# A smaller mask product, separate keys for the first transfers, and a planner without its correction tables

## The chip, the cores and the metric

The kernel runs on one core of a Trainium2 chip. The metric is the device time of one execution in microseconds (us). Three executions of the kernel before took 328.57, 328.97 and 334.71 us, median 328.97. One more execution was taken with the hardware profiler; all rows below are from it.

## The reference

Two independent layers are computed and put side by side into an output of 2048 rows and 1280 columns, all in bf16.

```python
# A: 640 channels, 2048 steps
k_shift = sum(k_pad[:, t:t+S, :] * shift_k[:, ks-1-t] for t in range(4))
kv = k_shift * v
y = causal_long_convolution(kv, ssm_k)      # written with rfft/irfft of length 4096
a = q * (y + kv * ssm_D)
# B: 32 heads of 20, 4 segments of 512 steps
for s in range(4):
    p = softmax(qs @ ks.T * scale + causal_mask)
    a_dot = p @ vs
    a_mem = (phi(qs) @ M) / (phi(qs) @ z + 1e-6)      # phi(t) = t+1 if t>0 else exp(t)
    outs.append(g * a_mem + (1 - g) * a_dot)
    M, z = M + phi(ks).T @ vs, z + phi(ks).sum()
b = concat(outs) @ wo
return concat([a, b], axis=-1)
```

## The kernel before, in words

**Part A** runs over five blocks of 128 channels (`a_chunks(dp)`). For each block the filter `sk` and the keys are loaded, `sk` is turned by products with the identity (`turn`), the keys are shifted by products with `skd` (`kshift`), both are transformed by products with the table `Wf` (`fwd`, evicted by ScalarE into `F`), combined by VectorE (`bfly`, `pointwise`, `ybfly`: products and sums over tiles `Xh`, `Kh`, `S`), and transformed back by products with `Wi` (`inverse`), whose result VectorE multiplies by q into `outa` and GpSimd's queue writes out.

**Part B** runs over eight units: segment `s` = u // 2 and half of the heads u % 2. A unit's projection (`b_proj_chunks(u)`) multiplies `xT` (x transposed by a DMA) by `wqkv` for four tiles of 128 tokens, in the order K, Q, V. ScalarE casts K and Q into `KQ`; SyncE's queue (SP) transposes them by DMA into `KT` and `QT`, eight transposes per unit. `bound` then takes the largest absolute key on VectorE (`kam`), multiplies on TensorE, and writes a row `bT` into `QT` by a DMA. `mem` updates the state `Mbd`. A unit's attention (`b_attn_chunks(u)`) runs over four groups of four heads (`attn(g)`). For each group three score blocks are made one after the other in the one PSUM tile `st` (four banks, one per head); ScalarE takes the exponential of each into `ET`, of which there are three; VectorE multiplies the diagonal blocks of the first two by `cmask`; TensorE multiplies `ET` by `Va` into the one bank `o`; VectorE divides. When both halves of a segment are through, `o_s` is transposed by DMAs (`outt`) and multiplied by `wo` (`outproj`, evicted into `outb`).

The third score block holds key tile 3 in columns 0 to 127 and key tile 2 in columns 128 to 383. Before its score products, four products of the identity with `nmask` (two causal masks of -30000 and a block of zeros, 384 columns) put the mask into the four banks; the score products add to them. A score product works on 32 of TensorE's rows (`tile_position`), so that the four heads of a group run beside each other; I call these four a quartet.

**The order.** No call is issued as it is written. A recorder (`Proxy`, `Recorder.add`) collects the calls as operations, each with a key: `("A", block, stage)`, `("P", unit, stage)` for projections, `("T", unit, stage)` for attention and output, `("load", name)`, `("beta",)`, and `("const",)` for everything issued at set-up. Consecutive products into one bank are one operation. `Recorder.price` gives each an assumed duration. `plan` schedules them: it runs a list scheduler forward in time, then backward, up to seven forward runs, and keeps the shortest by its own durations. The first run's priorities are the length of the work behind an operation plus a correction per key from the table `BIAS`; in the later runs an eighth of that correction is kept. `HOLD` names, per key, a time before which a transfer isn't issued; in the later runs it moves the times that the planner derives for loads. `emit` then issues everything in the chosen order, so all instructions have the line of `emit` in the profile. Each engine, and each engine's DMA queue, works through its own instructions in that order. PSUM has one `st` of four banks, three banks `ab` and one bank `o`.

Of the kernel before, what the change touches and what calls it, by code (L numbers as in the profile page):

```python
# [12 lines left out]
bf16 = mybir.dt.bfloat16  # L13
# [80 lines left out]
class Recorder:  # L94
# [87 lines left out]
    def price(self, op, method, out, ins, kw):  # L182
        n = int(np.prod(list(out.shape)[1:]))
        two = lambda a: mybir.dt.size(a.dtype) == 2
        if method == "matmul":
            if "tile_position" in kw:
                op.dur += n / 2.4 * 0.33 + (200.0 if not op.dur else 0.0)
            else:
                op.dur += max(n / 2.4 + 2.5, 27.0)
# [15 lines left out]
        elif op.eng == "DVE":  # L205
            op.stall = 115 if method == "reciprocal" else 0
            fast = all(two(a) and a.space != bass.MemoryType.PSUM and int(a.ap[-1][0]) == 1 for a in [out] + ins)
            if method == "tensor_tensor":
                op.dur = n / (1.92 if fast else 0.96) + 60
            elif method == "tensor_reduce":  # L210
                op.dur = int(np.prod(list(ins[0].shape)[1:])) / 0.96 + 60
            elif method == "reciprocal":
                op.dur = 67 + 6.1 * n
            else:
                op.dur = n / (3.84 if fast else 1.9) + 60
            op.lat = 150.0
        else:
            op.dur, op.lat = 100 + n / 1.2, 200.0
# [231 lines left out]
class K3:  # L450
    def __init__(self, ctx, tc, A_q, A_k, A_v, A_shift_k, A_ssm_k, A_ssm_D, B_x, B_wq, B_wk, B_wv, B_wo, B_beta, out):
# [20 lines left out]
        def const(name, arr, dt, eng=nc.gpsimd):  # L472
            t = c.tile(list(arr.shape), dt, name=name)
# [8 lines left out]
        def wload(engs, half):  # L482
            def f():
                for i, (w, eng) in enumerate(zip((B_wk, B_wq, B_wv), engs)):
                    eng.dma_start(out=self.wqkv[:, :, half, i, :], in_=w.rearrange("(cc p) j -> p cc j", p=128)[:, :, 320 * half:320 * half + 320])
# [6 lines left out]
        }  # L492
        self.skc = c.tile([128, 5, 4], bf16, name="skc")
        nc.sync.dma_start(out=self.skc[:], in_=self.shift_k.rearrange("(c p) t -> p c t", p=128))
        self.ident = const("ident", np.eye(128).astype(BF16_NP), bf16, nc.sync)
        bt = self.bt = c.tile([128, H], bf16, name="bt")
# [4 lines left out]
        self.nmask = const("nmask", np.concatenate([(cmask_np.astype(np.float32) - 1) * 30000.0] * 2 + [np.zeros((128, 128), np.float32)], axis=1).astype(BF16_NP), bf16)  # L501
        self.epsrow = const("epsrow", eps_np, f32)

        self.KQ = c.tile([128, 2, 2, 16, 32], bf16, name="KQ")
        self.PK = c.tile([128, 4, 16, 32], bf16, name="PK")
# [45 lines left out]
    def a_chunks(self, dp):  # L551
# [22 lines left out]
        def load_kv():  # L574
            vt = st["vt"] = self.ring("vt", [128, 4, 4, 128])
            for b in range(4):
                nc.sync.dma_start(out=vt[:, b], in_=self.v[512 * b:512 * b + 512, dsl].rearrange("(p c) d -> p c d", c=4))
            kr = st["kr"] = self.ring("kr", [128, 4, KPAD + 512])
            nc.gpsimd.memset(kr[:, :, 0:KPAD], 0.0)
            for c in range(4):  # L580
                nc.sync.dma_start_transpose(out=kr[:, c, KPAD:KPAD + 512], in_=self.k[:, dsl].rearrange("(r c) d -> r c d", c=4)[:, c, :])
            skd = st["skd"] = self.ring("skd", [128, 4, 128])
# [191 lines left out]
    def b_attn_chunks(self, u):  # L774
# [6 lines left out]
        def attn(g):  # L781
            def f():
# [5 lines left out]
                for spec, e0, step in ((((0, 0),), 0, -1), (((1, 0),), 512, 1), (((3, 0), (2, 128)), 896, -1)):  # L788
                    st = self.bank("st")
                    masked = e0 == 896  # L790
                    if masked:
                        for hl in range(4):
                            nc.tensor.matmul(st[:, hl, 0:384], lhsT=self.ident[:], rhs=self.nmask[:], start=True, stop=False)
                    for (kc, c0) in spec:
                        for hl in range(4):
                            rows = slice(32 * hl, 32 * hl + 32)
                            nc.tensor.matmul(st[:, hl, c0:c0 + L - 128 * kc], lhsT=KT[rows, g, 128 * kc:128 * kc + 128], rhs=QT[rows, g, 128 * kc:L],
                                             start=not masked, stop=(not masked or kc == 2), tile_position=(32 * hl, 0))
# [82 lines left out]
    ('A', 0, 0): 157004, ('A', 0, 1): 10101, ('A', 0, 10): -7597, ('A', 0, 11): 3913, ('A', 0, 12): 33761, ('A', 0, 13): -3728, ('A', 0, 14): 5624,  # L881
    ('A', 0, 15): 88348, ('A', 0, 16): 230629, ('A', 0, 17): -8128, ('A', 0, 18): -5757, ('A', 0, 19): 10830, ('A', 0, 2): 8829, ('A', 0, 20): 4481,
    ('A', 0, 21): 1304, ('A', 0, 22): -3994, ('A', 0, 23): 145, ('A', 0, 24): -576, ('A', 0, 25): -2524, ('A', 0, 26): -1099, ('A', 0, 27): -2858,
    ('A', 0, 3): 16866, ('A', 0, 4): -698, ('A', 0, 5): -458, ('A', 0, 6): 389434, ('A', 0, 7): 607, ('A', 0, 8): 3517, ('A', 0, 9): -8145,
    ('A', 1, 0): -1731, ('A', 1, 1): 3601, ('A', 1, 10): -137531, ('A', 1, 11): -176854, ('A', 1, 12): -7874, ('A', 1, 13): -16279, ('A', 1, 14): 10588,
    ('A', 1, 15): 2905, ('A', 1, 16): -7, ('A', 1, 17): -2655, ('A', 1, 18): -2590, ('A', 1, 19): -1545, ('A', 1, 2): 1649, ('A', 1, 20): 40028,
    ('A', 1, 21): 1391, ('A', 1, 22): 3816, ('A', 1, 23): -2584, ('A', 1, 24): -7, ('A', 1, 25): -2923, ('A', 1, 26): 731, ('A', 1, 27): 396,
    ('A', 1, 3): 395, ('A', 1, 4): -322, ('A', 1, 5): 12977, ('A', 1, 6): 7861, ('A', 1, 7): -1057, ('A', 1, 8): -201, ('A', 1, 9): 261,
    ('A', 2, 0): -69696, ('A', 2, 1): -2356, ('A', 2, 10): -15708, ('A', 2, 11): 257, ('A', 2, 12): -55, ('A', 2, 13): 1762, ('A', 2, 14): 6674,
    ('A', 2, 15): 491, ('A', 2, 16): 243, ('A', 2, 17): -2104, ('A', 2, 18): 175, ('A', 2, 19): 3992, ('A', 2, 2): -3416, ('A', 2, 20): 250546,  # L890
    ('A', 2, 21): -2544, ('A', 2, 22): -615, ('A', 2, 23): -563, ('A', 2, 24): -3861, ('A', 2, 25): 952, ('A', 2, 26): 5253, ('A', 2, 27): -3491,
    ('A', 2, 3): -2503, ('A', 2, 4): -4457, ('A', 2, 5): 2480, ('A', 2, 6): 5034, ('A', 2, 7): -2075, ('A', 2, 8): 243, ('A', 2, 9): -346,
    ('A', 3, 0): -36045, ('A', 3, 1): 546, ('A', 3, 10): 150040, ('A', 3, 11): -1390, ('A', 3, 12): 2538, ('A', 3, 13): -590, ('A', 3, 14): 898,
    ('A', 3, 15): 3192, ('A', 3, 16): -3627, ('A', 3, 17): -3799, ('A', 3, 18): -1242, ('A', 3, 19): 12597, ('A', 3, 2): 492, ('A', 3, 20): -88007,
    ('A', 3, 21): 959, ('A', 3, 22): -5393, ('A', 3, 23): -3393, ('A', 3, 24): -1459, ('A', 3, 25): 91621, ('A', 3, 26): 73805, ('A', 3, 27): 18751,
    ('A', 3, 3): -1299, ('A', 3, 4): -1550, ('A', 3, 5): -2302, ('A', 3, 6): 1825, ('A', 3, 7): 239, ('A', 3, 8): -4198, ('A', 3, 9): 1989,
    ('A', 4, 0): 7225, ('A', 4, 1): 3377, ('A', 4, 10): -14537, ('A', 4, 11): 1258, ('A', 4, 12): -875, ('A', 4, 13): -2828, ('A', 4, 14): -1432,
    ('A', 4, 15): 3521, ('A', 4, 16): 902, ('A', 4, 17): 30, ('A', 4, 18): -2548, ('A', 4, 19): 10489, ('A', 4, 2): -568, ('A', 4, 20): 140696,
    ('A', 4, 21): -37556, ('A', 4, 22): -7189, ('A', 4, 23): -383007, ('A', 4, 24): -253753, ('A', 4, 25): 258369, ('A', 4, 26): -29115,
    ('A', 4, 27): -5191, ('A', 4, 3): 2201, ('A', 4, 4): -1131, ('A', 4, 5): 2555, ('A', 4, 6): 1762, ('A', 4, 7): -3359, ('A', 4, 8): 33,  # L900
    ('A', 4, 9): 2421, ('P', 0, 0): -9006, ('P', 0, 1): -12460, ('P', 0, 2): 205250, ('P', 0, 3): -6447, ('P', 0, 4): -7691, ('P', 0, 5): -9283,
    ('P', 0, 6): -6859, ('P', 1, 0): -6426, ('P', 1, 1): 14273, ('P', 1, 2): 27558, ('P', 1, 3): 4361, ('P', 1, 4): 30756, ('P', 1, 5): -9966,
    ('P', 2, 0): 206102, ('P', 2, 1): 2606, ('P', 2, 2): 55679, ('P', 2, 3): 222011, ('P', 2, 4): -5184, ('P', 2, 5): 322, ('P', 2, 6): 3855,
    ('P', 3, 0): 539, ('P', 3, 1): 12770, ('P', 3, 2): 6817, ('P', 3, 3): -2388, ('P', 3, 4): -3574, ('P', 3, 5): -34190, ('P', 4, 0): 93926,
    ('P', 4, 1): -2574, ('P', 4, 2): 3367, ('P', 4, 3): 8133, ('P', 4, 4): 941, ('P', 4, 5): -8595, ('P', 4, 6): 1265, ('P', 5, 0): 5809,
    ('P', 5, 1): -6587, ('P', 5, 2): -4494, ('P', 5, 3): 470, ('P', 5, 4): -11, ('P', 5, 5): -3290, ('P', 6, 0): -201866, ('P', 6, 1): -7579,
    ('P', 6, 2): -924, ('P', 6, 3): -2026, ('P', 6, 4): -925, ('P', 6, 5): -12309, ('P', 7, 0): 2422, ('P', 7, 1): 8081, ('P', 7, 2): 239694,
    ('P', 7, 3): -9934, ('P', 7, 4): -5328, ('T', 0, 0): 4372, ('T', 0, 1): 13516, ('T', 0, 2): 39780, ('T', 0, 3): 10861, ('T', 1, 0): 325,
    ('T', 1, 1): 45, ('T', 1, 2): -7524, ('T', 1, 3): 3438, ('T', 1, 4): 76084, ('T', 1, 5): 45, ('T', 1, 6): 45, ('T', 1, 7): 45, ('T', 1, 8): 40,
    ('T', 2, 0): 5369, ('T', 2, 1): 2730, ('T', 2, 2): 2984, ('T', 2, 3): -984, ('T', 3, 0): 8766, ('T', 3, 1): 10627, ('T', 3, 2): 4686,  # L910
    ('T', 3, 3): -33267, ('T', 3, 4): -70352, ('T', 3, 5): 4037, ('T', 3, 6): -909, ('T', 3, 7): -537, ('T', 3, 8): -78941, ('T', 4, 0): -662,
# [94 lines left out]
```

The softmax here doesn't subtract the row's maximum and nothing guards it: scores larger than these inputs give would overflow.

## Time and profile before

| | value |
|---|---|
| median of three runs | 328.97 us |
| profiled execution: whole time, span of the program | 332.81 us, 331.0 us |
| instructions | 8829 |
| ScalarE exponentials `ET<-st` | 96, 154.9 us busy |
| TensorE projection products `ab<-wqkv,xT` | 480, 75.9 us busy |
| TensorE mask products `st<-nmask,ident`, 128x384 | 128, 26.4 us busy, mean 329 ns |
| TensorE score products `st<-QT,KT` | 512, 34.8 us busy, mean 303 ns |

A mean duration is that of one instruction from its start to its end. TensorE's products overlap: the next starts while the one before still drains, so the distance from one start to the next is shorter than the duration. PE is TensorE, DVE VectorE, ACT ScalarE, POOL GpSimd, SP SyncE; SPq is SP's DMA queue.

### The profile page before, as it was taken

The page shows a single profiled execution, that of the slowest core. Times are in us where ns is not written, and L with a number is a line of the kernel's source. Part 1 is how long each engine was busy: PE and PEld are TensorE (multiplying, and loading weights), DVE is VectorE, ACT ScalarE, POOL GpSimd, SP SyncE. Part 2 cuts the span into 40 slices and gives each one's busy share as a digit, 9 for nine tenths or more (in the row PEclk, how much of TensorE's full clock was granted, in tenths as well). Part 3 has the DMA queues.
Part 4 walks back from the last instruction along what each step waited for, and adds up shares of the span by engine and source line. Part 5 has one row for each costly group of instructions (what it writes and reads, how often), then busy time and mean ns, then how long its engine had stood idle before and what let it go on. Part 6 is the DMA issues. An engine that isn't in the chain of part 4 may idle for free. (4 is left out here: it accounts for less than half of the span.)

```text
span 331.0 us, 8829 instructions
## 1 busy us (share of the span) xinstructions
PE 287.2 (87%) x3673; PEld 199.6 (60%) x3674; DVE 272.7 (82%) x455; ACT 266.0 (80%) x351; POOL 30.4 (9%) x58
## 2 busy tenths in 40 slices
PE   0498899989999995999999995999989997897982
PEld 0375766666767674566857662676765664564641
DVE  0016859999998979999997597799999999999942
ACT  1176699799998998899898887878899999668711
POOL 5001100000000010000101010300010001330310
PEclk9998999999999999799999998999999999998998
DMA  8945954646405986813321669504303452324272
GB/s 251 224 95 125 253 95 94 124 125 111 81 2 141 201 136 155 209 50 81 70 59 53 119 135 188 139 6 77 66 20 69 60 79 60 98 49 126 66 138 79
DMA packets 97159, 35.65 MB, mean 108 GB/s; under 512 B 90000, under 2 KB 95168, under 8 KB 96864
## 3 DMA queue, kind: packets, MB, share of 16 engines
q1 hardware_dynamic: 94816, 30.01, 43.7%
q0 software_dynamic: 1872, 4.76, 5.5%
q8 instruction: 28, 0.46, 0.6%
q10 hardware_dynamic: 432, 0.34, 0.3%
q14 instruction: 11, 0.09, 0.1%
HBM read 13.46 MB, written 5.24 MB: 56 GB/s over the span
## 5 line engine op out<-in xcount | busy, mean ns | idle before, releaser
L441 ACT ACTIVATE ET<-st 128x1536 bf16<-128x1536 f32 (+1 forms) x96 | 154.9, 1614 | 23.1 <-PE st L441 22.4
L441 PE MATMUL ab<-wqkv,xT 128*128 128x320 bf16 x480 | 75.9, 304 | 13.3 <-DMA wqkv<-in_B_wk_dram 12.6
L441 PEld LDWEIGHTS <-xT 128*128 128x128 bf16 x480 | 45.1, 99 | 33.3 <-DMA xT<-in_B_x_dram 10.6
L441 PEld LDWEIGHTS <-ET 128*128 128x128 bf16 x1280 | 42.3, 96 | 10.2 <-issue 6.6
L441 ACT CAST F<-ab 128x512 bf16<-128x512 f32 x80 | 45.4, 615 | 2.3 <-PE ab L441 1.6
L441 PE MATMUL o<-Va,ET 128*128 128x21 bf16 x1280 | 44.1, 173 | 2.3 <-DVE o L441 1.9
L441 PE MATMUL st<-QT,KT 32*128 32x128 bf16 (+3 forms) x512 | 34.8, 303 | 8.7 <-ACT ET L441 8.5
L441 ACT CAST KQ<-ab 128x320 bf16<-128x320 f32 x64 | 28.0, 461 | 14.9 <-PE ab L441 14.4
L441 DVE TENSOR_TENSOR S<-S 128x2048 bf16<-128x2048 bf16 (+1 forms) x40 | 37.0, 941 | 0.0
L441 PEld LDWEIGHTS <-Wf 128*128 128x128 bf16 x320 | 28.1, 97 | 11.8 <-issue 7.9
L441 PE MATMUL st<-nmask,ident 128*128 128x384 bf16 x128 | 26.4, 329 | 2.8 <-ACT ET L441 2.7
L441 PEld LDWEIGHTS <-KT 32*128 32x128 bf16 x512 | 11.8, 91 | 28.2 <-issue 26.3
L441 PE MATMUL ab<-wo,oT 128*128 128x320 bf16 (+1 forms) x140 | 22.4, 300 | 4.1 <-ACT outb L441 3.5
L441 PE MATMUL ab<-kT,Wf 128*128 128x256 bf16 x160 | 23.6, 273 | 0.9 <-ACT F L441 0.2
L441 POOL DMA_DIRECT2D out_dram<-outa x20 | 15.3, 767 | 93.0 <-DVE outa L441 85.3
L441 DVE TENSOR_TENSOR o<-o,rr 128x320 bf16<-128x320 f32 x48 | 23.2, 484 | 0.5
L441 PE MATMUL ab<-vt,Wf 128*128 128x256 bf16 x160 | 22.0, 273 | 1.3 <-DVE vt L441 1.2
L441 DVE TENSOR_TENSOR ET<-ET,cmask 128x1024 bf16<-128x1024 bf16 x32 | 21.6, 675 | 1.6 <-ACT ET L441 1.6
L441 DVE TENSOR_TENSOR S<-Xh,Kh 128x4096 bf16<-128x4096 bf16 x10 | 22.8, 2278 | 0.0
L441 PEld LDWEIGHTS <-oT 128*128 128x128 bf16 x160 | 14.1, 100 | 13.7 <-issue 6.5
L441 PE MATMUL ab<-skd,kr 128*128 128x128 bf16 x320 | 22.0, 227 | 0.3 <-DVE vt L441 0.2
L441 DVE RECIPROCAL rr<-o 128x16 f32<-128x16 f32 (+1 forms) x64 | 15.3, 239 | 7.3 <-PE o L441 7.3
(70 smaller groups left out, 402.7 us busy)
## 6 DMA issues: line engine op xcount, KB each, us to landing
sk<-in_A_ssm_k_dram SPq DMA_DIRECT2D x5, 512.0 KB, 3.9
vt<-in_A_v_dram SPq DMA_DIRECT2D x20, 128.0 KB, 3.2
qd<-in_A_q_dram SPq DMA_DIRECT2D x20, 128.0 KB, 3.3
out_dram<-outa POOLq DMA_DIRECT2D x20, 128.0 KB, 2.6
out_dram<-outb POOLq DMA_DIRECT2D x12, 160.0 KB, 2.6
Wf<-c_wf SPq DMA_DIRECT2D x1, 1024.0 KB
Wi<-c_wi SPq DMA_DIRECT2D x1, 1024.0 KB
wqkv<-in_B_wq_dram SPq DMA_DIRECT2D x2, 400.0 KB, 5.5
```

Source lines behind the costliest of these rows:

```text
L441: f(*[fix(a) for a in args], **{k: fix(v) for k, v in kw.items()})
```

## The change

Three things change.

1. The mask product covers columns 0 to 255 only, and `nmask` loses its block of zeros. The third score block's product for key tile 2 is split: columns 128 to 255 add to the mask, columns 256 to 383 start their own sum. So each group has four mask products of 256 columns in place of 384, and three quartets of 128 columns in place of one of 128 and one of 256.
2. At set-up each constant's transfer gets a key of its own, as do the three weight loads of each half, the transposing load `kr` and the small product `skd` of each block of A. Before, they shared the key of what stood around them.
3. The planner's assumed durations change (score products 0.26 in place of 0.33 per column, VectorE 8 ns more for each operation), and the tables `BIAS` and `HOLD` are empty: no correction and no hold is left for any key. So the order of the whole program is planned anew.

```diff
             if "tile_position" in kw:
-                op.dur += n / 2.4 * 0.33 + (200.0 if not op.dur else 0.0)
+                op.dur += n / 2.4 * 0.26 + (200.0 if not any("tile_position" in c[3] for c in op.calls[:-1]) else 0.0)
...
                 op.dur = n / (3.84 if fast else 1.9) + 60
+            op.dur += 8
...
         def const(name, arr, dt, eng=nc.gpsimd):
+            self.rec.key = ("const", name)
...
                 for i, (w, eng) in enumerate(zip((B_wk, B_wq, B_wv), engs)):
+                    self.rec.key = ("load", f"w{half}", i)
...
-        self.nmask = const("nmask", np.concatenate([(cmask_np.astype(np.float32) - 1) * 30000.0] * 2 + [np.zeros((128, 128), np.float32)], axis=1).astype(BF16_NP), bf16)
+        self.nmask = const("nmask", np.concatenate([(cmask_np.astype(np.float32) - 1) * 30000.0] * 2, axis=1).astype(BF16_NP), bf16)
...
+            self.rec.key = ("A", dp, "kr")
             kr = st["kr"] = self.ring("kr", [128, 4, KPAD + 512])
...
+            self.rec.key = ("A", dp, "skd")
             skd = st["skd"] = self.ring("skd", [128, 4, 128])
...
-                            nc.tensor.matmul(st[:, hl, 0:384], lhsT=self.ident[:], rhs=self.nmask[:], start=True, stop=False)
-                    for (kc, c0) in spec:
+                            nc.tensor.matmul(st[:, hl, 0:256], lhsT=self.ident[:], rhs=self.nmask[:], start=True, stop=False)
+                    parts = [(kc, c0, 0, L - 128 * kc) for kc, c0 in spec] if not masked else [(3, 0, 0, 128), (2, 128, 0, 128), (2, 128, 128, 256)]
+                    for (kc, c0, a, b) in parts:
                         for hl in range(4):
                             rows = slice(32 * hl, 32 * hl + 32)
-                            nc.tensor.matmul(st[:, hl, c0:c0 + L - 128 * kc], lhsT=KT[rows, g, 128 * kc:128 * kc + 128], rhs=QT[rows, g, 128 * kc:L],
-                                             start=not masked, stop=(not masked or kc == 2), tile_position=(32 * hl, 0))
+                            nc.tensor.matmul(st[:, hl, c0 + a:c0 + b], lhsT=KT[rows, g, 128 * kc:128 * kc + 128], rhs=QT[rows, g, 128 * kc + a:128 * kc + b],
+                                             start=not masked or a > 0, stop=not masked or kc == 2, tile_position=(32 * hl, 0))
...
 BIAS = {
-    ('A', 0, 0): 157004, ('A', 0, 1): 10101, ('A', 0, 10): -7597, ('A', 0, 11): 3913, ('A', 0, 12): 33761, ('A', 0, 13): -3728, ('A', 0, 14): 5624,
...
 HOLD = {
-    ('A', 0, 27): 160307, ('A', 1, 0): 46314, ('A', 1, 10): 26348, ('A', 1, 20): 123338, ('A', 1, 25): 181398, ('A', 2, 0): 21093, ('A', 2, 20): 214889,
...
```

## The prediction

> **What bounds it now.** I read the page's busy times first.
>
> ```profile
> span 331.0 us, 8829 instructions
> ...
> PE 287.2 (87%) x3673; PEld 199.6 (60%) x3674; DVE 272.7 (82%) x455; ACT 266.0 (80%) x351; POOL 30.4 (9%) x58
> ```
>
> TensorE, VectorE and ScalarE are all at 80 to 87%: none has room to take much more, and none alone is the end. So I cut the span at the eight times at which ScalarE starts a unit's first exponential (columns: stretch, its length, then busy time and count of each engine):
>
> ```profile
> 36.10:71.70 35.60, 32.86 (x445) 23.67 (x446) 31.24 (x58) 32.77 (x46) 1.22 (x3) 1.00 0.62 129
> 71.70:106.00 34.30, 32.42 (x460) 23.54 (x458) 33.13 (x61) 32.93 (x44) 0.66 (x2) 1.00 0.40 84
> 106.00:141.60 35.60, 31.17 (x373) 21.48 (x372) 32.78 (x51) 32.32 (x43) 2.83 (x4) 0.95 0.92 182
> 141.60:176.30 34.70, 33.31 (x484) 23.52 (x482) 34.24 (x61) 33.08 (x45) 0.94 (x2) 1.00 0.27 55
> 176.30:216.90 40.60, 36.45 (x451) 24.35 (x450) 30.76 (x49) 33.19 (x45) 5.74 (x9) 0.96 0.61 128
> 216.90:252.30 35.40, 34.36 (x478) 25.23 (x477) 35.19 (x57) 31.81 (x40) 1.66 (x2) 1.00 0.27 54
> 252.30:286.70 34.40, 31.74 (x399) 20.75 (x397) 33.62 (x56) 31.20 (x41) 3.15 (x5) 1.00 0.38 69
> 286.70:331.00 44.30, 33.11 (x431) 21.62 (x432) 31.96 (x58) 24.31 (x26) 8.73 (x13) 0.93 0.35 88
> ```
>
> In each unit but the last the busiest engine fills 90 to 99% of the stretch, and it changes: TensorE in units 0 and 4 (from 36.10 and 176.30), VectorE in the others, with ScalarE never more than 3.5 us behind. The last stretch also holds the drain. So one engine's saving counts only where that engine ends the stretch, and it counts that the planner keeps all three fed.
>
> The PE timeline of one third score block (start, length, instructions):
>
> ```profile
> 211.97 0.81 PE L441 MATMUL st<-nmask,ident 128*128 128x384 bf16 x4
> 212.71 0.34 PE L441 MATMUL st<-QT,KT 32*128 32x128 bf16 x8
> 212.99 0.61 PE L441 MATMUL ab<-kT,Wf 128*128 128x256 bf16 x4
> 213.43 1.06 PE L441 MATMUL ab<-skd,kr 128*128 128x128 bf16 x16
> ```
>
> The mask's four products start 0.74 us before the score products behind them (211.97 to 212.71). The two quartets, of 128 and 256 columns, take 0.28 us until the next full product starts. Below, four products of 256 columns take 0.44, 109 ns each.
>
> The timeline of the start:
>
> ```profile
> 0.74 0.35 SPq L441 DMA_DIRECT2D Wf<-c_wf  x1
> 1.14 0.44 SPq L441 DMA_DIRECT2D sk<-in_A_ssm_k_dram  x1
> 1.64 5.73 SPq L441 DMA_TRANSPOSE xT<-in_B_x_dram  x1
> ...
> 8.04 0.52 SPq L441 DMA_DIRECT2D wqkv<-in_B_wk_dram  x1
> ...
> 12.56 2.83 PE L441 MATMUL ab<-wqkv,xT 128*128 128x320 bf16 x10 [12.56 <-DMA wqkv<-in_B_wk_dram]
> ...
> 14.60 1.22 SPq L441 DMA_TRANSPOSE KT<-KQ  x1
> ...
> 23.97 2.57 SPq L441 DMA_TRANSPOSE QT<-KQ  x2
> ...
> 36.14 1.88 ACT L441 ACTIVATE ET<-st 128x2048 bf16<-128x2048 f32 x1 [3.83 <-PE st L441]
> ```
>
> SP issues Wf and sk, 1.5 MB, ahead of x, whose issue then takes 5.73 us. The first product runs at 12.56, the last Q transpose of unit 0 is issued by 26.54, and attention starts at 36.14. VectorE has hardly run by then.
>
> **The change, part by part.** *The mask.* One product of 384 columns starts 162 ns before the next of its kind, one of 256 columns 109 ns. Four of them: 162*3 + 258 before, 109*3 + 205 after, so 212 ns less; 258 and 205 are with the change to 32-row products, which costs 96 ns and occurs as often as before. The split adds a quartet: the quartet of 128 columns starts 56 ns before the next quartet (32 of 32 cases), two of them 112, for one of 256 columns at 107. Net 207 ns per group, 32 groups: **6.6 us** less TensorE time. The 128 added weight loads run under the products, as the loads of every quartet do (that distance of 56 ns has four loads in it); if they did not, by their row's 91 ns each, four side by side, 32*0.09 = 3 us come back.
>
> The Trainium skill speaks against the split: "TensorEngine Tiling (Array Packing)", section "Instruction Overhead", gives each matmul about 60 cycles of overhead. Paid by each added product alone it would be an estimated 25 ns * 128 = 3.2 us and leave 3.4 of the 6.6; the 56 ns of the whole quartet say it isn't paid that way here.
>
> *The first transfers.* The new program's order has x first on SP, then the weights for K, Q and V, then Wf, sk, ident. x's issue starts at 0.74 in place of 1.64. With nothing ahead it takes between 3.08 us (the issue of x at 202.02) and 5.73, so K's weights are issued at 3.8 to 6.5; they landed 4.5 us after issue before (8.04 to 12.56), behind more traffic. First product at 8.3 to 11.0: 1.5 to 4.2 earlier, I take 2.8. The eight transposes with one `kr` among them fill 14.60 to 26.54 on SP without a hole; the new order has the same nine and the 0.5 us issue of `skc` in between. So attention starts 2.8 - 0.5 = **2.3 us earlier**, with ends 3.7 and 0: nothing, if Wf and sk, now 1.5 us of queue or more later, make A's first products late on TensorE. Nothing covers the start; a gain there is kept as far as the later stretches are limited by their own work. `nmask` shrinks from 96 to 64 KB on POOL's queue, first used 9 us after it lands (31.7, 40.9): nothing.
>
> *The order.* The empty tables change every engine's order, so I compare how evenly the two programs feed the engines. Each instruction of the new order gets the distance to the next start that the trace shows for its kind (lower quartile): 136 ns for a projection product, 25 for an `o` product, 109 for 256 columns, 1.77 and 1.34 us for exponentials of 2048 and 1536, 0.31 and 0.47 for casts of 320 and 512, 2.20, 1.13 and 0.60 for VectorE's work on 4096, 2048 and 1024. Totals: PE 265.1 before and 258.5 after, ACT 252.3, DVE 264.4 in both. Per unit (first exponential to the next unit's) PE/ACT/DVE are
>
> - before: 30.8/31.6/32.2, 31.5/31.7/32.3, 28.3/31.3/30.1, 31.7/32.1/31.7, 33.5/31.6/34.6, 32.9/30.3/35.6, 30.2/29.7/28.9, 29.6/22.5/25.7
> - after: 30.4/30.2/23.1, 28.7/32.8/33.9, 30.1/30.5/32.4, 30.1/30.4/34.1, 31.7/34.3/42.7, 34.8/31.6/28.9, 30.6/29.7/31.1, 26.5/21.2/24.3
>
> The sum of each unit's largest is 257.9 before and 265.9 after: **8.0 us more**. In unit 0 VectorE gets 23.1 us of work in place of 32.2, and unit 4 has to make it up with 42.7. Cut by pairs of units it is 257.9 to 258.2, +0.3; cut by two groups it is 282.3 to 278.7, -3.6. The mask's saving is in these sums: it remains where PE is largest after (units 5 and 7, 0.8 us each, a little in unit 0). Which cut holds depends on how far one engine runs ahead of another. Three `ET` and one `st` allow about three groups, so a surplus is not carried across two units in full, nor is it lost at every border. The two nearest cuts are the unit and the pair, and I take the middle of +8.0 and +0.3: **+4.2 us**, ends -3.6 and +8.0.
>
> What the planner could still win or lose shows in ScalarE's waits (total, times, longest):
>
> ```profile
> ACT ET L441 <- PE st L441: 22.4, 30, 3.8
> ```
>
> These 22.4 us in 30 waits are the exponentials that had no scores; a change of order by -3.6 or +8.0 is a sixth or a third of them.
>
> Sum: -2.3 + 4.2 = +1.9 us. The profiled execution took 332.81 us (span 331.0, 1.8 around it), 3.84 above the median of 328.97, so this goes on the median: 328.97 + 1.9 = **331 us**.
>
> **The rivals.** *Faster: the start and the saving both come through.* The start gains its 3.7 and the finer cut holds, -3.6: -7.3, 321.7. For it: PE has 6.6 us less everywhere and unit 7, the one where PE is largest by far, loses 3 us of it (29.6 to 26.5). Against: PE is the largest after in only three units of eight. 0.2.
>
> *Slower: VectorE's debt.* VectorE is left idle in unit 0, where the new order puts 23.1 us beside 30.4 of PE. At unit 1's start it has done 36.9 us in place of 45.4, with TensorE at 46.0. From there to unit 6's start it has 172.0 us of work in place of 164.4. That stretch took 180.6 us (71.7 to 252.3) for the 164.4, 1.10 us per us, so the 7.6 more cost 8.3; with no gain at the start, 337.3. It decides if VectorE stays over 95% busy in units 1 to 4 after its idle unit 0. For it: VectorE has no hole longer than 1.2 us from 48 to 182 us now, so it can't make up a debt. Against: the pair cut. 0.27.
>
> *Slower by a queue: Wi ahead of unit 3's Q transposes.* The new order issues Wi (1 MB) between the first K and Q transpose of a unit's four pairs; before, it stood ahead of them. At the 251 GB/s of the page's first slice it occupies the DMA engines for 4.2 us, and ScalarE and the bound wait for `QT`: 328.97 + 1.9 + 4.2 = 335. 0.08.
>
> **The numbers.** Forecast 331, chance 0.45: by its terms' inner ends from 326 (start 3.7, order +0.3) to 335 (start 0, order +6). The whole range runs from 321, the fast rival, to 340, the slow one and 3 us of loads that show: about one in ten is left on each side. Two per cent, about what a measurement of this kernel tells from no change, is 322.4 and 335.5. Faster by more: over half of the first rival, 0.13. Slower by more: the debt's 0.27 and a part of the queue's, 0.32. Between: 0.55.
>
> **What would show it.** Mask: four `nmask` products of 256 columns 0.53 us ahead of the score products, then 56 ns per quartet; about 6.6 us less PE busy time. Start: first product at 8.3 to 11, first exponential at 33 to 36. Order: VectorE under 75% in unit 0 and over 95% in unit 4, whose length exceeds 43 us. The forecast is wrong if attention starts no earlier, if VectorE is well fed in unit 0, or if one wait longer than 4 us stands in the chain that has no counterpart now.

## The result, and the profile after

| | before | after |
|---|---|---|
| median of the runs taken together | 330.39 us (4 runs, 328.57 to 334.71) | 342.94 us (4 runs, 341.84 to 343.65) |
| ratio, 95% interval | | 1.0396 [1.0317, 1.0475] |
| profiled execution: time, span | 332.81, 331.0 us | 343.65, 341.9 us |

The changed kernel is slower by 4%, 12.6 us; the prediction of 331 us, with a range to 340, is too low. In some executions of a kernel the clock is lower and the time some per cent longer: the medians here are over all executions, the ratios over those without this. The page of the changed kernel first: span, busy times, and the granted TensorE clock in 40 slices (tenths); the last row is the clock of the kernel before.

```profile
span 341.9 us, 9096 instructions
...
PE 290.0 (85%) x3801; PEld 204.1 (60%) x3802; DVE 273.7 (80%) x455; ACT 265.6 (78%) x351; POOL 30.7 (9%) x58
...
PEclk9996999999699998998899998999998999995787
```

```profile
PEclk9998999999999999799999998999999999998998
```

TensorE's busy time rose by 2.8 us although its work shrank, and the clock row has eleven slices of 40 at 8 or less, where the kernel before has five. Next the same cut as in the prediction, at each unit's first exponential; the column after POOL's is the granted clock.

```profile
33.04:67.71 34.67, 32.59 (x474) 25.23 (x474) 23.13 (x49) 31.26 (x42) 0.15 (x1) 0.98 0.64 138
67.71:104.24 36.53, 31.78 (x418) 21.02 (x417) 35.03 (x58) 33.95 (x46) 0.51 (x1) 0.91 0.32 67
104.24:143.97 39.73, 33.76 (x485) 24.33 (x484) 32.49 (x54) 31.34 (x39) 1.72 (x3) 0.96 0.73 135
143.97:181.65 37.68, 34.34 (x445) 23.10 (x444) 35.82 (x63) 32.27 (x41) 3.21 (x6) 0.91 0.44 78
181.65:220.95 39.30, 34.88 (x443) 25.32 (x441) 35.48 (x50) 35.53 (x49) 3.22 (x7) 0.96 0.70 140
220.95:261.22 40.27, 38.08 (x534) 28.11 (x533) 38.97 (x63) 33.60 (x45) 3.01 (x4) 0.96 0.37 65
261.22:294.65 33.43, 31.69 (x443) 22.12 (x440) 32.67 (x54) 30.64 (x42) 4.84 (x7) 1.00 0.36 78
294.65:341.88 47.23, 32.82 (x429) 21.04 (x428) 28.88 (x54) 22.88 (x23) 7.46 (x11) 0.78 0.31 76
```

Attention starts 3.1 us earlier (33.04 against 36.14). Then the units change by -0.9, +2.2, +4.1, +3.0, -1.3, +4.9, -1.0 and +2.9 us. The loss is spread over five units. Single units also vary from execution to execution: unit 4 of the kernel before took 40.6 us in this one, but 36.4 to 37.0 in the three runs below that follow its order, so the -1.3 is no gain. In unit 2, one of the worst, no engine is near full: TensorE 85%, VectorE 82%, ScalarE 79%. That is time spent in waits. In units 1, 3 and 5 VectorE is at 95 to 97%, and it is busy there for 1.9, 1.6 and 3.8 us more than before.

From TensorE's side the 10.9 us of span are: first product 4.7 us earlier (7.85 in place of 12.56), idle time behind it 39.1 us in place of 26.3 (+12.8), busy time +2.8. The waits that grew most (total, times, longest), and behind them the second one as it was before:

```profile
ACT ET L442 <- PE st L442: 27.2, 28, 5.3
PE st L442 <- ACT ET L442: 25.8, 30, 3.2
...
DVE rr L442 <- PE o L442: 16.9, 18, 2.3
...
DVE kam L442 <- DMA KT<-KQ: 6.2, 4, 1.9
...
ACT KQ L442 <- DMA KT<-KQ: 4.0, 2, 2.4
```

```profile
PE st L441 <- ACT ET L441: 12.4, 19, 2.5
```

Before, the five rows held 22.4, 12.4, 7.3 and 1.0 us, and the last didn't exist. TensorE waiting for an exponential, so that the one score tile comes free, has doubled. The longest one, in ScalarE's and TensorE's timelines (start, length, instruction, and in brackets the idle time before it with its releaser):

```profile
82.14 1.57 ACT L442 ACTIVATE ET<-st 128x1536 bf16<-128x1536 f32 x1
83.47 2.03 ACT L442 ACTIVATE PqT<-QT 128x2048 bf16<-128x2048 bf16 x1
85.27 2.00 ACT L442 ACTIVATE ET<-st 128x2048 bf16<-128x2048 f32 x1
```

```profile
83.76 0.40 PE L442 MATMUL st<-QT,KT 32*128 32x512 bf16 x4 [0.45 <-ACT ET L442]
87.32 0.51 PE L442 MATMUL st<-QT,KT 32*128 32x384 bf16 x4 [3.16 <-ACT ET L442]
87.80 1.49 PE L442 MATMUL ab<-wqkv,xT 128*128 128x320 bf16 x5
89.22 1.87 PE L442 MATMUL ab<-tq,A 128*16 128x512 bf16 x4
```

The scores of 83.76 are ready by 84.2, but ScalarE is in the 2.03 us of `PqT`, a step of the next unit that stands between two exponentials. The exponential starts at 85.27, and the next scores at 87.32: the scores' products stand first in TensorE's order, nothing behind them may pass, and TensorE idles 3.16 us. The kernel before has its six `PqT` between exponentials too. Counted over both traces by what ScalarE did just before the exponential, the waits behind a `PqT` grew from 5.0 to 9.0 us, those behind ScalarE's steps for a projection from 0.3 to 5.5, those where one exponential followed another directly from 1.1 to 6.6; the others fell from 6.0 to 4.7. What a wait does to the clock is seen by windows (stretch, length, busy times, granted clock):

```profile
82.30:85.70 3.40, 1.11 (x21) 0.74 (x19) 3.37 (x5) 3.40 (x4) 0.00 (x0) 1.00 0.60 159
85.70:92.50 6.80, 5.18 (x45) 2.25 (x44) 6.73 (x11) 5.26 (x7) 0.00 (x0) 0.50 0.32 82
92.50:95.90 3.40, 3.40 (x58) 2.29 (x57) 2.12 (x6) 2.68 (x4) 0.51 (x1) 1.00 0.01 5
```

After 3.4 us in which TensorE was busy for a third, it runs 6.8 us at half clock. The clock record of the whole trace has ten phases at half clock, 53.4 us in all, against five and 18.8 us before (the last one of each lies behind TensorE's last product). Counting half of TensorE's busy time in them as lost, that is an estimated 20.2 us against 6.7. The profiled execution has the lowest mean clock of the changed kernel's four, 0.925; the others have 0.939 to 0.945.

### The profile page after: what moved, and what is told of

The parts are those of the page before. It is cut to its first block, busy times and chain, and to the rows that moved or that the text cites. A ratio compares the mean times of both kernels' runs of the same rounds, so it can differ in the third digit from the quotient of the medians.

```text
span 341.9 us, 9096 instructions
## 1 busy us (share of the span) xinstructions
PE 290.0 (85%) x3801; PEld 204.1 (60%) x3802; DVE 273.7 (80%) x455; ACT 265.6 (78%) x351; POOL 30.7 (9%) x58
## 3 DMA queue, kind: packets, MB, share of 16 engines
q1 hardware_dynamic: 94816, 30.01, 44.4%
## 4 chain that ended last, share of the span: by engine, by line
PE 50%; ACT 21%; DVE 13%; DMA 9%; issue 4%; SPq 2%; DVEq 0%; ACTq 0%
PE ab L442 34%; ACT ET L442 11%; PE st L442 9%; PE o L442 6%; DMA KT<-KQ 5%; ACT F L442 4%; DVE S L442 3%; ACT PqT L442 2%; SPq L442 2%; DVE kam L442 2%; DVE ET L442 2%; DMA wqkv<-in_B_wk_dram 1%; ACT KQ L442 1%; DVE o L442 1%; DMA QT<-KQ 1%
## 5 line engine op out<-in xcount | busy, mean ns | idle before, releaser
L442 PE MATMUL ab<-wqkv,xT 128*128 128x320 bf16 x480 | 77.9, 308 | 8.7 <-DMA wqkv<-in_B_wk_dram 7.8
L442 PE MATMUL st<-QT,KT 32*128 32x128 bf16 (+2 forms) x640 | 36.5, 285 | 16.5 <-ACT ET L442 16.3
L442 ACT CAST F<-ab 128x512 bf16<-128x512 f32 x80 | 44.1, 616 | 1.5 <-PE ab L442 0.8
L442 PEld LDWEIGHTS <-Wf 128*128 128x128 bf16 x320 | 29.6, 100 | 9.3 <-issue 3.5
L442 PEld LDWEIGHTS <-KT 32*128 32x128 bf16 x640 | 13.9, 93 | 35.0 <-issue 33.0
L442 PE MATMUL st<-nmask,ident 128*128 128x256 bf16 x128 | 20.9, 290 | 8.4 <-ACT ET L442 8.4
L442 PE MATMUL ab<-kT,Wf 128*128 128x256 bf16 x160 | 24.6, 292 | 0.4
L442 DVE TENSOR_REDUCE kam<-KT 128x4 f32<-128x2048 bf16 x8 | 18.3, 2284 | 6.4 <-DMA KT<-KQ 6.2
L442 PE MATMUL ab<-S,Wi 128*128 128x256 bf16 x160 | 23.2, 296 | 0.2 <-DVE outa L442 0.2
L442 PEld LDWEIGHTS <-kr 128*128 128x128 bf16 x320 | 19.8, 102 | 5.5 <-issue 5.1
```

Source lines behind the costliest of these rows:

```text
L442: f(*[fix(a) for a in args], **{k: fix(v) for k, v in kw.items()})
```

## The experiments

The kernels were timed in groups, each group beside the kernel before on the same chip; each ratio is to those runs. In several kernels the planner's list is replaced by one written into the kernel, taken from the other kernel or put together from both, with this edit:

```diff
     def plan(self, bias, hold, passes, slack):
+        self.order = [self.ops[i] for i in FIXED]
+        self.slot = {id(o.bank): FIXED_SLOTS[o.idx] for o in self.order if o.new}
+        return 0
```

**The order and the mask, one at a time.** First, the changed kernel's code issued in the order of the kernel before, operation by operation:

> The order of the kernel before, operation by operation, with the smaller mask product and the split quartet. Theory A (the new order costs the time; the mask edit saves TensorE time): PE loses 6.6 us of products, PE idle time grows by a part of it, and the time is 324 to 329 us against about 330 for the kernel before. Rival B (the mask edit itself costs, by the added quartet and its weight loads): 334 us or more, half-speed clock as in the changed kernel (mean granted clock about 0.93).

Second, the kernel before issued in the changed kernel's order:

> The order of the changed kernel, operation by operation, with the old mask product of 384 columns. Theory A: as slow as the changed kernel or slower, 342 to 349 us, since the order stays and PE gets 6.6 us more. Rival B: near the kernel before, 328 to 334 us.

| | median | ratio, 95% interval | TensorE idle | waits st <- ET | half clock |
|---|---|---|---|---|---|
| old order, new mask | 329.89 us (10 runs) | 0.9922 [0.9882, 0.9961] | 29.8 us | 10.3 | 14.6 |
| new order, old mask | 343.94 us (4 runs) | 1.0313 [1.022, 1.0406] | 38.6 us | 24.0 | 35.9 |

So the order carries the whole loss. The mask edit by itself is a small gain, 0.8% (329.89 us lies just over the 324 to 329 foretold, on a chip where the kernel before took 332.37). On the new order no gain of it is seen: 1.0313 without it and 1.0396 with it, intervals that overlap. Units 2 and 5 with the new mask in the old order (compare 39.73 and 40.27 above):

```profile
104.19:139.26 35.07, 30.52 (x389) 21.19 (x388) 32.13 (x51) 32.41 (x43) 2.83 (x4) 0.95 0.88 185
...
210.78:246.31 35.53, 33.88 (x494) 25.47 (x493) 35.32 (x57) 31.88 (x40) 1.60 (x2) 1.00 0.28 54
```

**The start.** The kernel before with only its first eight transfers on SP in the new sequence (x, the weights for K, Q and V, `Wf`, `sk`, `ident`, `skc`):

> The order of the kernel before, but the first eight transfers on SP's queue in the changed kernel's order (x, the three weights, Wf, sk, ident, skc). If the gain at the start is kept: first product at about 7.9 us in place of 12.6, first exponential about 3 us earlier, time 326 to 328 us. If it is taken back by VectorE's or ScalarE's own work behind it: 329 to 331 us, with the first exponential earlier all the same.

Measured: 332.95 us (329.81, 330.80, 335.10 and 335.15) beside 332.37 of the kernel before (13 runs, 330.83 to 337.70). Two of the four lie below every run of the kernel before and two above most of them, so whether there is a gain of some 2 us can't be told from this run. In its profile attention starts at 35.2 us, 1.0 earlier and not 3.1. That start moves by itself, though: the old order with the new mask and the old first transfers had it at 34.8.

**Both edits without the new order.** The old order, the new mask and the new first transfers:

> The order of the kernel before with both edits that do what the change says: the smaller mask product and the first eight transfers in the changed kernel's order. If the mask's 2.5 us (0.8% on the old order) is all there is: ratio to the kernel before 0.990 to 0.994. If the start adds its 1 to 3 us on top once TensorE has less to do: 0.983 to 0.989.

Measured: 328.28 us, ratio 0.9878 [0.9816, 0.994]. The ratio lies in the range for a start that adds its part, but the interval holds the other range too, so a gain of 1 to 2 us from the start is neither shown nor excluded. This is the best version found and beats both kernels. It computes by the same code as the changed kernel, so the two orders differ by 1.0396/0.9878 = 1.052, some 17 us.

**The empty tables.** The kernel before with `BIAS = {}` and `HOLD = {}` and nothing else changed:

> The kernel before with both correction tables empty and nothing else changed (old keys, old assumed durations, old mask). Theory A1 (the emptied tables cost the time): 338 to 350 us. Rival A2 (the new keys and assumed durations mislead the planner, the tables are worth little): 326 to 334 us.

Measured: 340.34 us, ratio 1.0234 [1.0164, 1.0304], with waits st <- ET of 15.6 us and 25.1 us of half clock. By the ratios emptying the tables alone costs over half of the loss, 2.3 of 4.0 per cent. What the new keys and assumed durations add to it wasn't tried by itself. The reverse is the changed kernel with both tables refilled (`HOLD` in the same way); nothing else of it is altered:

```diff
 BIAS = {
-   
+    ('A', 0, 'kr'): -3700, ...
 }
```

> The changed kernel with its two tables filled again: a random search changed a few corrections and holds at a time and kept what shortened the planner's own total, from 323.4 us (empty tables) to 315.2. Nothing else differs from the changed kernel. Theory (the empty tables cost the time, through an order in which more operations wait): the other two parts of the change keep their worth, and with a plan 8.1 us shorter the time is 331 us or less, ratio to the kernel before 0.985 to 1.00, exponentials that TensorE waits for (st <- ET) 15 us or less, half-speed clock 25 us or less. Rival (the planner's durations are wrong, above all the new ones, and its total says little): 336 or more, with waits of 20 us and half-speed clock of 30 us or more as in the changed kernel.

> As the run before, from another random search that ended at the same planned total, 315.2 us, with another order. Theory (the planned total carries over): within 3 us of the run before. Rival (the total says little): the two differ by more than 4 us, or both are at 336 or more.

> The changed kernel with the tables of the kernel before, each new key given the number of the key that it was split from. The planner's total is 321.2 us, 2.1 less than with empty tables. Theory (the planned total carries over): 338 to 342. Rival (the old numbers hold what the chip needs and the planner's durations don't see): 334 or less.

| changed kernel with | planner's own total | median | ratio, 95% interval | half clock | TensorE idle |
|---|---|---|---|---|---|
| empty tables (the change) | 323.4 us | 342.94 us | 1.0396 [1.0317, 1.0475] | 53.4 us | 39.1 us |
| the old numbers | 321.2 us | 343.86 us | 1.0385 [1.0322, 1.0448] | 42.9 us | 40.6 us |
| refilled, first search | 315.2 us | 336.08 us | 1.0151 [1.0091, 1.0212] | 24.1 us | 38.9 us |
| refilled, second search | 315.2 us | 332.90 us | 1.0046 [1.0, 1.0092] | 22.4 us | 33.8 us |

By the ratios refilled tables take back 2.4 and 3.5 of the 4.0 per cent, so most of the loss can be taken back by corrections and holds alone. The theory asked for 331 us or less and the two within 3 us of each other. They are at 336.1 and 332.9, 3.2 apart: the planner's total points the right way but is blunt by a few us, and neither order reaches the old one (328.28 with the same code). In the first of them the waits st <- ET (12.9 us) and the half clock (24.1) came down as far as the theory asked and the time didn't (336.1, which its rival had), so these two aren't the whole loss. The old numbers in the new tables bring nothing, 343.86 us where 338 to 342 or 334 and less were foretold. The second search's waits and its units 1 to 3:

```profile
PE st L442 <- ACT ET L442: 11.9, 17, 1.8
```

```profile
76.61:112.45 35.84, 32.70 (x476) 24.15 (x475) 30.76 (x58) 31.68 (x42) 1.72 (x3) 1.00 0.47 101
112.45:147.61 35.16, 29.86 (x424) 20.87 (x423) 32.62 (x52) 31.60 (x40) 2.22 (x4) 0.95 0.62 118
147.61:182.25 34.64, 32.10 (x478) 23.91 (x477) 30.24 (x56) 31.53 (x40) 2.06 (x3) 1.00 0.43 97
```

The waits for exponentials are halved and no unit is over 36 us until the last. This order starts attention late, at 41.75 us, with more of part A ahead of it (VectorE is busy for 18.5 us by then, 11.2 in the changed kernel), and still ends 10 us sooner.

**The clock in the last unit.** The changed order with 50 products of `ident` and a slice of `Wf` added in TensorE's gaps behind nine operations of the last unit; they go into a free bank, and nothing reads them:

```diff
+            if o.idx in FILL:
+                slot, n = FILL[o.idx]
+                for _ in range(n):
+                    self.real.tensor.matmul(self.slots["ab"][slot][:], lhsT=self.ident[:], rhs=self.Wf[:, 0, 0, :], start=True, stop=True)
```

> The changed kernel's order with 50 products more in the last unit: each a product of the identity with 512 columns of Wf into a bank that is free, placed on TensorE ahead of the nine waits longer than 0.2 us after 300 us (10.8 us of products at full clock); nothing reads them. Theory C (TensorE's idle spells drop its clock to half, and that costs time in the last unit, 13.7 us at half speed from 307.5): the half-speed time after 300 us falls from 22.7 us to 10 or less, the last unit from 47.2 us to 43 to 45, the time to 339 to 341 us. Rival (the clock is only a sign; the last unit waits for ScalarE's exponentials anyway, or the added products stand in the way): 342 us or more.

The stretch around 307 us in the changed kernel, and with the fillers:

```profile
300.70:307.50 6.80, 4.17 (x75) 2.97 (x68) 6.77 (x9) 5.81 (x6) 2.59 (x4) 1.00 0.63 163
307.50:321.20 13.70, 10.10 (x118) 5.90 (x118) 10.64 (x20) 6.28 (x5) 0.75 (x1) 0.50 0.05 13
```

```profile
300.00:307.00 7.00, 7.00 (x86) 4.57 (x83) 6.66 (x10) 5.50 (x7) 2.19 (x4) 1.00 0.48 130
307.00:321.00 14.00, 13.81 (x182) 7.96 (x178) 12.75 (x23) 7.96 (x6) 1.57 (x3) 1.00 0.18 50
```

The fillers keep the clock up, and the last unit takes 44.4 us in place of 47.2, about what the kernel before takes (44.3). The same order without fillers took 45.4 us for this unit in the run with the third buffer below, so 1 to 3 us of it are the clock's. Over the whole kernel it isn't seen: 342.14 us where 339 to 341 were foretold, ratio 1.0276 [1.018, 1.0372], an interval that overlaps the changed kernel's. The fillers touch only one unit, and in this execution attention started 1.35 us later (34.39), which they can't have caused.

**A third buffer for K and Q.** ScalarE's casts into `KQ` wait 4.0 us for transposes that still read the slot. The changed order with three slots (two more lines follow from it):

```diff
-        self.KQ = c.tile([128, 2, 2, 16, 32], bf16, name="KQ")
+        self.KQ = c.tile([128, 3, 2, 16, 32], bf16, name="KQ")
...
-                KQ = self.KQ[:, tci % 2]
+                KQ = self.KQ[:, tci % 3]
```

> The changed kernel's order with KQ three deep in place of two, so that ScalarE's cast of a token tile no longer waits for the transposes of the tile before last. Theory T (bunched projections wait for their transposes through KQ): ScalarE's wait for KT transposes, 4.0 us, goes, and the time falls by 2 to 4 us, to 339 to 341 us. Rival (the eight transposes of a unit take 1.25 us each on SP whatever the buffer): the wait moves to VectorE's kam, 6.2 us now, and the time stays within 1 us of the changed kernel.

Measured: 341.33 us, ratio 1.028 [1.0199, 1.0362]: by the interval no difference from the changed kernel. The wait moved on to the next step:

```profile
DVE kam L447 <- DMA KT<-KQ: 6.9, 5, 1.9
...
ACT PqT L447 <- DMA QT<-KQ: 5.5, 3, 4.7
```

ScalarE no longer waits at `KQ`, but the transposes still come one after the other, and the steps that need them wait instead (`PqT` 5.5 us in place of 4.0).

**VectorE's debt.** The old order up to unit 1's first exponential, then the new one:

> The changed kernel's instructions in the order of the kernel before up to the first exponential of unit 1, and from there in the changed kernel's order (21 operations moved a little, where a bank was not free). So unit 0 has its work of part A on VectorE again and no debt is left for units 1 to 5. Debt theory: the loss is gone, 333 us or less, and units 1 to 5 take at most 184 us together as in the kernel before (180.6). Theory of waits (the later order itself feeds the engines late, through exponentials and transposes): 337 to 342, units 1 to 5 together 189 us or more, TensorE's wait for exponentials over 18 us.

Measured: 355.33 us, ratio 1.0712 [1.0642, 1.0782], slower than either theory said. The time is lost at the seam, in unit 1: from 74 to 91 us eleven groups of projection products stand there, eight of which wait 0.2 to 1.1 us for a cast of ScalarE, while attention goes on slowly. Its units 1 to 3:

```profile
72.93:117.03 44.10, 31.88 (x416) 20.20 (x414) 28.74 (x54) 33.50 (x44) 0.51 (x1) 0.92 0.21 49
117.03:157.46 40.43, 33.82 (x485) 24.37 (x484) 32.35 (x54) 31.40 (x39) 1.72 (x3) 0.96 0.72 133
157.46:194.26 36.80, 32.21 (x445) 21.97 (x444) 35.53 (x63) 32.09 (x41) 3.21 (x6) 1.00 0.49 80
```

VectorE was busy for 28.74 of unit 1's 44.10 us, so it isn't late when unit 2 starts. Units 2 to 5, which follow the changed kernel's order, still take 156.3 us (40.4, 36.8, 39.0, 40.1) beside 157.0 in the changed kernel and 146.3 before. So arrears from unit 0 aren't needed to make those units long. But the run keeps the work of those units as the changed kernel has it (unit 2 has the same 485, 54 and 39 instructions on TensorE, VectorE and ScalarE), and that is more for VectorE: busy 141.2 us in units 2 to 5 beside 133.0 before. Whether the work moved there is what costs, it doesn't test.

**Which part of the order.** Both orders bring the 96 exponentials in the same sequence, so each operation can be placed by where it stands between two exponentials. First part A as in the new order and part B as in the old, then the reverse, then only the projections as in the new:

> The changed kernel's instructions; the order is put together from both: every operation has a place relative to the 96 exponentials (which come in the same sequence in both orders); part A, with its loads, stands where the changed kernel has it, part B where the kernel before has it. If the loss comes from where part B's projections stand (a unit's projections bunched, the transposes behind them late): 334 or less. If it comes from where part A stands (VectorE's debt, or what A takes from TensorE at the wrong time): 337 or more. If only the two together cost: 334 or less here and in the next run.

> The reverse: part A stands where the kernel before has it, part B where the changed kernel has it. Theory of the projections: 337 or more, with TensorE's wait for exponentials over 18 us. Theory of part A: 334 or less, wait 13 us or less. If the two only cost because they don't fit each other: both mixed orders are at 338 or more.

> As the kernel before in everything but the projections of the eight units (their products, casts, transposes, bounds and states), which stand where the changed kernel has them. Theory of the projections: within 3 us of the run before this one, 336 or more. Otherwise 334 or less.

Measured: 398.28, 396.99 and 389.79 us, ratios 1.200 [1.192, 1.209], 1.188 [1.173, 1.203] and 1.167 [1.155, 1.178]. Here the first run meets the bound for part A, the second that for the projections; together they meet the one for parts that don't fit each other, though nothing had priced some 60 us. Two orders that take some 330 and 343 us give 390 to 398 us when their parts are mixed, though every operation keeps its place from one of them, but for small shifts where no bank was free. The third run meets neither of its bounds (within 3 us of the second, or 334 and less). The part at fault can't be told this way. That the two parts have to fit into each other's gaps would explain it, but no run shows it.

## Why the prediction was wrong

**The mask: right in the stream.** Two groups in TensorE's timeline, the old order with the new mask, then the changed kernel:

```profile
214.75 0.84 PE L447 MATMUL ab<-wqkv,xT 128*128 128x320 bf16 x5
215.42 0.60 PE L447 MATMUL st<-nmask,ident 128*128 128x256 bf16 x4
215.96 0.23 PE L447 MATMUL st<-QT,KT 32*128 32x128 bf16 x4
```

```profile
217.09 0.60 PE L442 MATMUL st<-nmask,ident 128*128 128x256 bf16 x4
217.62 0.35 PE L442 MATMUL st<-QT,KT 32*128 32x128 bf16 x12
217.90 1.53 PE L442 MATMUL ab<-wo,oT 128*128 128x320 bf16 x10
```

Scores follow the masks by 0.53 us as foretold, and three quartets take 0.28. From the first mask product to what follows the scores the median of 32 groups is 1021 ns before and 811 after, 210 less (207 foretold): 6.7 us. In the old order 2.5 us of that reach the end (329.89 beside 332.37), as the prediction said that a saving counts only where TensorE ends the stretch.

**The start: right in place; whether it was kept isn't settled.** x's issue took 2.93 us, the first product ran at 7.85 (8.3 to 11.0 foretold, a little early) and the first exponential at 33.04 (33 to 36).

```profile
0.74 2.93 SPq L442 DMA_TRANSPOSE xT<-in_B_x_dram  x1
3.73 0.57 SPq L442 DMA_DIRECT2D wqkv<-in_B_wk_dram  x1
...
7.85 7.59 PE L442 MATMUL ab<-wqkv,xT 128*128 128x320 bf16 x45 [7.85 <-DMA wqkv<-in_B_wk_dram]
```

The -2.3 us were counted as kept. In the old order a gain from it is neither shown nor excluded (332.95 beside 332.37; 0.9878 with the mask beside 0.9922). The second refilled order starts attention nearly 9 us later (41.75) and still ends 10 us sooner than the changed kernel, so how early attention starts says little by itself: work of part A that isn't done before has to be done beside attention.

**The order: the step that failed.** "The two nearest cuts are the unit and the pair, and I take the middle of +8.0 and +0.3: +4.2 us, ends -3.6 and +8.0." If the start is worth nothing, the order with the mask's saving in it cost 12.6 us, three times the value and over its upper end; if its 3.1 us were kept, 15.7. The sums of each engine's work per unit are a lower bound: the busiest engine is taken to work without a gap. The rows give both parts: added up over the units, the busiest engine was busy for 277.2 us in place of 271.4, 5.8 more (half clock included), and the time in which it too stood still went from 23.5 to 31.6 us, 8.1 more. So the sums were nearly right, +5.8 where +4.2 was taken, and within their ends. What failed is the step from sums to time: the gaps had no term, and they were the larger part. They lie inside the units, where a step on one engine comes late for another's. In unit 2 the largest of the after sums was 32.4 us and the unit took 39.73; before, 31.3 and 35.60 for the same unit. The term needed the change in the waits, for which TensorE's idle time (+12.8 us) is one measure. The sums of work held no sign of the gaps, and the planner's totals, at 316.0 us for the kernel before and 323.4 for the changed one, gave 7.4 of the 12.6 us.

**The price list was taken at full clock.** Each instruction of the new order was costed at the distance that it had before, nearly all at full clock. That holds for the 6.6 us of the mask, but the new waits bring half-clock phases that by the estimate above lose 13.5 us of TensorE's time more than before (20.2 against 6.7). That would raise TensorE's busy time by 6.9 us with the mask's saving taken off; it rose by 2.8, so half of the busy time is too high a count. How much of it lies on the path isn't settled: in the last unit it was 1 to 3 us (the fillers), in the others no run tells.

**The rivals.** *VectorE's debt* had some of its signs: 67% busy in unit 0 (under 75% foretold), 95 to 97% in units 1, 3 and 5. Its condition, over 95% in all of units 1 to 4, failed in units 2 (82%) and 4 (90%), and unit 4 took 39.3 us and not over 43. Its price fits all the same: from unit 1's start to unit 6's VectorE was busy for 177.8 us in place of 166.1, and the stretch took 193.5 us in place of 180.6, 12.9 us for 11.7, or the 1.10 us per us that the rival reckoned with. In units 1, 3 and 5 VectorE's 1.9, 1.6 and 3.8 us more stand beside 2.2, 3.0 and 4.9 us of length; unit 2, with 4.1 us more and VectorE less busy than before (32.49 beside 32.78), it can't explain. No run moves VectorE's work alone, so this rival stands, as a part of the loss. *Wi on the queue* happened at its place and was smaller than priced. On SP's queue and ScalarE:

```profile
103.65 1.24 SPq L442 DMA_TRANSPOSE KT<-KQ  x1
104.94 0.57 SPq L442 DMA_DIRECT2D Wi<-c_wi  x1
...
108.99 1.57 SPq L442 DMA_TRANSPOSE KT<-KQ  x1
```

```profile
114.36 0.43 ACT L442 CAST KQ<-ab 128x320 bf16<-128x320 f32 x1 [2.37 <-DMA KT<-KQ]
```

The key transpose of 108.99 stands for 5.29 us in the chain that ended last, where the median landing of these transposes is 2.5 us after issue, and ScalarE waits 2.37 us for it, not 4.2. With 4.91 us for the one of 149.25, two such waits of over 4 us stand in the chain, one of the prediction's signs of being wrong. Whether they have a counterpart isn't known: the chain of the kernel before reaches back only to 203 us (its longest wait for a DMA is 3.80), and a key transpose took up to 4.6 us to land there too. Whether `Wi` or the queries' loads beside it slowed it wasn't tried. *The fast rival* needed fewer waits and got more.

**What stays open.** That the order carries the loss is shown; which placement in it costs most isn't. Waits for exponentials, late transposes, half clock and VectorE's work moved into units 1 to 5 appear together, and each single remedy (the fillers, the third buffer, unit 0's old order) left the time about where it was or made it worse.

## What to carry to other kernels

For a schedule of in-order engines the sum of work per stage says only what time a stage can't beat; the gaps come on top, here 8.1 us beside 5.8. When a change replans everything, run the literal edit in the old order as well, here 1.2% faster while the replanned kernel was 4% slower. And refill a planner's corrections whenever its keys or durations change; the old numbers were as good as none here.

## What the runs showed of the hardware

**A half-busy TensorE is enough for the half clock.** The clock record of the traces keeps to windows of 3.41 us. I took the full-clock windows of six traces (before, after, old order with new mask, old kernel with empty tables, old numbers, first refill), up to TensorE's last product, and sorted them by the share in which TensorE was busy:

| TensorE busy in the window | followed by half clock | not |
|---|---|---|
| under 50% | 20 | 0 |
| 50 to 70% | 13 | 26 |
| over 70% | 0 | 451 |

The longest single gap inside a window that led to it was 2.4 us, and most were 1 to 2 us. The Trainium skill, "TensorE: Matmul & The Clock Gate", section "Why this matters for your kernels", asks to avoid idle gaps of more than about 3 us between bursts; in these runs shorter gaps did the same, and the busy share sorts the windows at both ends; between 50 and 70% it doesn't decide. What half clock means is in two lines shown above: five projection products took 1.42 us to the next start at 87.80 in the changed kernel, 284 ns each, and 0.67 us at 214.75 in the old order with the new mask, 134 ns each.
